# Blockwise attention feeding routed experts on one Trainium2 core: disjoint output views for the scatters, queries stored contiguous in blocks of 64, second-layer weights in row pairs

## The chip, the cores and the metric

The program runs on one core of one Trainium2 chip. The engines of a core are TensorE (PE; its weight loads are shown apart, as PEld), VectorE (DVE), ScalarE (ACT), GpSimd (POOL) and SyncE (SP); 16 DMA engines move data between the memory in HBM and the on-chip memory SBUF. The metric is device time in microseconds (us), the median of several executions.

## The reference

The first part is attention over 8 batches and 8 heads with 576 tokens of 64 numbers, causal by blocks of 64 tokens. The second part sends each of the 4608 rows of the attention output through one of eight small two-layer networks (the experts), chosen by an integer per row.

```python
def _attn_ref(q, k, v):                       # 8, 8, 576, 64
    scores = (1.0 / np.sqrt(D)) * np.matmul(q, k.transpose(0, 1, 3, 2))
    mask = (pos[:, None] // 64) >= (pos[None, :] // 64)
    scores = np.where(mask, scores, -1e9)
    attn = np.exp(scores - max);  attn = attn / (sum + 1e-09)
    return np.matmul(attn, v)

x = attn_out.transpose(0, 2, 1, 3).reshape(4608, 512)
for e in range(8):                            # w1: 8, 512, 1024   w2: 8, 1024, 512
    mask = domain_id == e
    out[mask] = np.maximum(x[mask] @ w1[e], 0.0) @ w2[e]
```

## The kernel before

**Attention stage.** The work goes in 32 pairs (8 batches times 4 pairs of heads). Queries, keys and values come in as float32, two batches at a time after the first, by DMAs that POOL issues; POOL casts them to float16 (L112, L116, L130). Query token t of a batch, after the first 64, is loaded as `(p j)` with j = 4: a partition holds four neighbouring tokens. `emit_T` transposes each head's four slices on PE into a PSUM tile `PT` (L311), so that PT holds the tokens of slice j side by side: column n of slice j is token 4n + j. DVE copies PT into the SBUF tile `QK`. The keys are put back into token order by that copy (L317). The queries are copied as they lie, slice after slice (L315), and token order is made each time they are read:

```python
def q_cols(QK, h, n0, n1):
    return QK[h, 0].rearrange("p (j n) -> p n j", j=4)[:, n0 // 4 : n1 // 4, :]
```

Neighbouring elements of such a read lie 128 elements, 256 bytes, apart. The last 64 keys and the first 64 queries of a batch are a "tail", transposed apart by `emit_tail` (L329) into `QT`.

For every pair `emit_G` makes three groups of score matmuls: group 0 has 512 query columns, group 1 has 384 and 128, group 2 has 256 (all L341, by `mm_qk`) and the twelve 64-column edge blocks (L369). Each matmul exists twice, once for either head of the pair, on partitions 0 to 63 and 64 to 127, with outputs in different PSUM banks (or, for the edges, different partitions). ACT makes the exponential of each group (L347). The tile `ps` that the groups write has two buffers. `emit_P` and `emit_Q` then multiply the exponentials of the pair before by the values (L397, L402) into the one tile `po`; a column of ones gives the row sums; DVE takes the reciprocal (L418) and scales `po` into `x` (L419). On PE the order of a pair is: group 0, the transposes for the pair after next, group 1, P of the pair before, group 2, Q of the pair before. `po` has one buffer, so the next P waits for L419. All engine queues are in the order of the code; there is no planner.

SP stores `x` to `x_rows` in HBM, one batch at a time. Between the pairs, `loads(p)` lets POOL cast and issue DMAs: at p = 3 the casts of the next keys and the weight loads of expert 0, at p = 4 the cast of the tail tile `th` of batch 2, and so on; `emit_tail` for batch b + 1 is in pair 4b + 2. DVE meanwhile works out, a step per pair, where each row goes (`routing`, `inverse`); the 36 matmuls of `inverse` are L216. The result is `tok`: a list of rows for each expert, 40 lists of 128, in `tok[:, 0]` as numbers of output rows and in `tok[:, 1]`, limited to 4607, as rows to gather.

**Expert stage.** Each expert has room for 640 rows, in five blocks. POOL gathers the blocks by indirect DMAs (L539); PE transposes them (L551), multiplies by w1 (`mm1`, L565, 64 matmuls of 320 columns), ACT applies the relu (L570), PE multiplies by w2 (`mm2`, L579, 40 matmuls of 512 columns), DVE copies each block's result to one of six `osb` buffers (L583) and POOL scatters it by an indirect DMA into the rows of `out` (L584). The weights are cast to float16 by the DMAs that bring them (L135, L138), four pieces for each matrix. All scatters name the whole tensor `out` as their destination. POOL's queue in expert e is: five gathers for expert e + 2, then for each block its scatter and two weight pieces for expert e + 3 (for e up to 4). A last loop (L631) serves experts with over 640 rows; it runs no round on these inputs.

Of the kernel before, what the change touches and what calls it, by code (L numbers as in the profile page):

```python
# [7 lines left out]

F32 = mybir.dt.float32
# [8 lines left out]
def kernel(  # L18
# [10 lines left out]
    nc = tc.nc  # L29
# [107 lines left out]
    def w2_piece(w2h, w2_e, i):  # L137
        nc.gpsimd.dma_start(  # L138
            out=w2h[:, 2 * i : 2 * i + 2],
            in_=w2_e[256 * i : 256 * i + 256, :].rearrange("(c p) f -> p c f", p=128))  # L140

    def load_w1(pool, bufs, w1_e):
        w1h = pool.tile([128, 4, Fdim], F16, name="w1h", tag="w1h", bufs=bufs)
# [42 lines left out]
    def inverse(sb, pp, tag, pbufs, ncols, base, tok):  # L186
        ub = sb.tile([128, NJ], F16, name="ub", tag="ub")
        nc.vector.tensor_scalar(
            out=ub[:], in0=u_f[:], scalar1=base, scalar2=None, op0=ALU.subtract)
        inv = sb.tile([128, 3, ncols], F32, name="inv", tag="inv")  # L190
        yield
        for hf in range(2):
            js = slice(NH * hf, NH * hf + NH)
            L = sb.tile([128, 128, NH], F16, name="L", tag="L")
            Hh = sb.tile([128, 3, ncols, NH], F16, name="Hh", tag="Hh")
            sh = [128, ncols, NH]
            nc.vector.tensor_tensor(
                out=Hh[:, 0], in0=iota_x[:, 0:ncols],
                in1=ub[:, js].unsqueeze(1).to_broadcast(sh), op=ALU.is_equal)
            nc.vector.tensor_scalar(  # L200
                out=Hh[:, 1], in0=Hh[:, 0], scalar1=p_f[:, 0:1], scalar2=None,
                op0=ALU.mult)
            nc.vector.tensor_tensor(
                out=Hh[:, 2], in0=Hh[:, 0],
                in1=iota_h[:, js].unsqueeze(1).to_broadcast(sh), op=ALU.mult)
            yield
            for m in range(0, 128, 64):
                nc.vector.tensor_tensor(
                    out=L[:, m : m + 64], in0=iota_x[:, m : m + 64],
                    in1=lo_h[:, js].unsqueeze(1).to_broadcast([128, 64, NH]),  # L210
                    op=ALU.is_equal)
                yield
            ps = pp.tile([128, 512], F32, name=tag, tag=tag, bufs=pbufs)
            pv = ps[:, 0 : 3 * ncols].rearrange("p (a c) -> p a c", a=3)
            for j in range(NH):
                nc.tensor.matmul(out=pv, lhsT=L[:, :, j], rhs=Hh[:, :, :, j],  # L216
                                 start=(j == 0), stop=(j == NH - 1))
# [10 lines left out]
        nc.vector.tensor_tensor(  # L228
            out=tok[:, 0], in0=inv[:, 0], in1=inv[:, 1], op=ALU.add)
        nc.vector.tensor_scalar(  # L230
            out=tok[:, 1], in0=tok[:, 0], scalar1=float(N - 1), scalar2=None,
            op0=ALU.min)
        yield

    def slot_col(asb, r_f, d_f, w, u, nm):
# [68 lines left out]
    def emit_T(p):  # L304
        b, hp = divmod(p, HP)
        PT = aps.tile([128, 2, 4, 128], F16, name="PT", tag="PT", bufs=2)
        QK = asb.tile([128, 2, 512], F16, name="QK", tag="QK", bufs=3)
        for s, src in enumerate((qh[b % 4], kh[b % 4])):
            for j in range(4):
                for i in range(2):  # L310
                    nc.tensor.transpose(  # L311
                        out=PT[64 * i : 64 * i + 64, s, j, :],
                        in_=src[:, 2 * hp + i, 64 * j : 64 * j + 64],
                        identity=identh[:])
        nc.vector.tensor_copy(  # L315
            out=QK[:, 0].rearrange("p (j n) -> p j n", j=4), in_=PT[:, 0])
        nc.vector.tensor_copy(  # L317
            out=QK[:, 1].rearrange("p (n j) -> p n j", j=4),
            in_=PT[:, 1].rearrange("p j n -> p n j"))
        return QK  # L320

    def q_cols(QK, h, n0, n1):
        return QK[h, 0].rearrange("p (j n) -> p n j", j=4)[:, n0 // 4 : n1 // 4, :]


    def emit_tail(QT, b):
        PT = aps.tile([128, HP, 2, 64], F16, name="PT", tag="PT", bufs=2)
        for g in range(HP):
            nc.tensor.transpose(  # L329
                out=PT[:, g].rearrange("p s n -> p (s n)"),  # L330
                in_=th[b % 4][:, 2 * g : 2 * g + 2, :].rearrange("p h d -> p (h d)"),
                identity=identh[:])
# [5 lines left out]
    def mm_qk(o, QK, c):  # L338
        for i in range(2):
            h = slice(64 * i, 64 * i + 64)  # L340
            nc.tensor.matmul(  # L341
                out=o[:, i].rearrange("p (n j) -> p n j", j=4),
                lhsT=QK[h, 1, 128 * c : 128 * c + 128],
                rhs=q_cols(QK, h, 128 * c, 512), start=True, stop=True)

    def emit_exp(o, i):
        nc.scalar.activation(out=o, in_=i, func=AF.Exp, scale=0.125)  # L347
# [1 line left out]
    def emit_G(g, st):  # L349
        QK = st["QK"]  # L350
        ps = aps.tile([128, 2, 512], F32, name="ps", tag="ps", bufs=2)
        if g == 0:
            mm_qk(ps[:], QK, 0)
            st["A1"] = asb.tile([128, 2, 512], F16, name="A1", tag="A1", bufs=2)
            emit_exp(st["A1"][:], ps[:])
        elif g == 1:
            mm_qk(ps[:, :, 0:384], QK, 1)
            mm_qk(ps[:, :, 384:512], QK, 3)
            st["A2"] = asb.tile([128, 2, 512], F16, name="A2", tag="A2", bufs=2)
            emit_exp(st["A2"][:], ps[:])  # L360
        else:
            mm_qk(ps[:, :, 0:256], QK, 2)
            for m in range(6):
                n0 = 128 * min(m, 4)
                c0 = 256 + 64 * (m % 3)
                QT = st["QT"][:, st["p"] % HP]
                for i in range(2):
                    h = slice(64 * i, 64 * i + 64)
                    nc.tensor.matmul(  # L369
                        out=ps[h, m // 3, c0 : c0 + 64].rearrange(  # L370
                            "p (n j) -> p n j", j=4),
                        lhsT=QK[h, 1, n0 : n0 + 64] if n0 < 512 else QT[h, 1],
                        rhs=q_cols(QK, h, n0 - 64, n0) if n0 else QT[h, 0].rearrange(
                            "p (n j) -> p n j", j=4),
                        start=True, stop=True)
# [182 lines left out]
    def mm1(xT, w1h):  # L558
        hT = msb.tile([128, 8, CAP], F16, name="hT", tag="hT", bufs=2)
        hw = CAP // 2  # L560
        for fc in range(8):
            ph = mps.tile([128, 2, 512], F32, name="ph", tag="ph", bufs=2)
            for dc in range(4):
                for i in range(2):
                    nc.tensor.matmul(  # L565
                        out=ph[:, i, 0:hw],
                        lhsT=w1h[:, dc, 128 * fc : 128 * fc + 128],
                        rhs=xT[:, dc, hw * i : hw * i + hw],
                        start=(dc == 0), stop=(dc == 3))
# [5 lines left out]
    def mm2(hT, w2h, tok, todo=()):  # L575
        for blk in range(NB):
            po = mps.tile([128, 512], F32, name="po", tag="po", bufs=2)
            for fc in range(8):
# [3 lines left out]
            osb = msb.tile([128, DM], F32, name="osb", tag="osb", bufs=6)  # L582
            nc.vector.tensor_copy(out=osb[:], in_=po[:])  # L583
            nc.gpsimd.indirect_dma_start(  # L584
                out=out,
                out_offset=bass.IndirectOffsetOnAxis(
                    ap=tok[:, 0, blk : blk + 1], axis=0),
                in_=osb[:], in_offset=None, bounds_check=N - 1, oob_is_err=False)
# [3 lines left out]
    def tok_of(e):  # L592
        return tok0[:, :, NB * e : NB * e + NB]
# [21 lines left out]
    for e in range(E):  # L615
# [14 lines left out]
    n_it = nc.values_load(n_i[0:1, 0:1], min_val=0, max_val=E * (N // CAP))  # L630
    with tc.For_i(0, n_it, 1) as it:  # L631
# [9 lines left out]
        for f in todo:  # L641
            f()
        hT = mm1(transpose_x(gather(tok)), w1h)
        mm2(hT, w2h, tok)


# [28 lines left out]
```

## Time and profile before

| | us |
|---|---|
| median of 3 runs | 456.5 (453.43 to 457.91) |
| the profiled execution | 451.2 |
| its span, first to last instruction | 449.2 |
| PE busy | 370.9 (83%) |
| POOL busy | 220.0 (49%) |
| DVE busy | 158.3 (35%) |
| ACT busy | 144.8 (32%) |

The row of an engine in the timeline gives the start, the busy time of a merged group of instructions, engine, line, operation, output and inputs, shape and count, and in brackets how long the engine sat idle before it and what ended that. A start minus the start of the next group is the time that a group holds the engine; matmuls are pipelined, so that the duration shown of one is longer than the time to the next. The gathers begin at 229.13 us; what lies before is the attention stage, what lies behind the expert stage.

### The profile page before, as it was taken

How to read it: one execution, taken by the hardware profiler on the slowest of the kernel's cores; microseconds unless marked ns; L12 is line 12 of the kernel's file. 1: busy time of each engine (PE TensorE's matmuls, PEld its weight loads, DVE VectorE, ACT ScalarE, POOL GpSimd, SP SyncE). 2: the span in 40 equal slices, each digit the busy share in tenths (PEclk: the TensorE clock that was granted, in tenths of full speed). 3: DMA queues.
4: the chain of work that ended last, by engine and by line, in shares of the span. 5: the costliest groups of instructions: out<-in, count | busy, mean ns of one | idle time of the engine just before them, and what ended most of it. 6: DMA issues, size and time to landing. Idle time of an engine off the chain costs nothing. (4 is left out here: it accounts for less than half of the span.)

```text
span 449.2 us, 7273 instructions
## 1 busy us (share of the span) xinstructions
PE 370.9 (83%) x3014; PEld 210.1 (47%) x3014; DVE 158.3 (35%) x302; ACT 144.8 (32%) x196; POOL 220.0 (49%) x252
## 2 busy tenths in 40 slices
PE   2879969999999999999718999897978969699300
PEld 1445535655555555555405565554453625446100
DVE  7849764444444434353210415121212122131100
ACT  1535433525454544455303150413040401304000
POOL 9869787745853100000048655647575464632220
PEclk9999999999999999999999999999896959989855
DMA  9999998953999010101035999694957869311210
GB/s 240 284 251 294 224 212 288 269 135 89 350 197 198 1 55 1 54 2 54 1 99 117 191 221 181 142 175 126 180 132 165 140 145 177 105 72 64 77 70 13
DMA packets 33635, 65.03 MB, mean 145 GB/s; under 512 B 4734, under 2 KB 19582, under 8 KB 33600
## 3 DMA queue, kind: packets, MB, share of 16 engines
q0 software_dynamic: 25424, 57.42, 55.4%
q1 hardware_dynamic: 7376, 6.72, 5.4%
q8 instruction: 25, 0.41, 0.4%
q10 hardware_dynamic: 800, 0.39, 0.3%
q14 instruction: 10, 0.08, 0.1%
HBM read 67.15 MB, written 15.20 MB: 183 GB/s over the span
## 5 line engine op out<-in xcount | busy, mean ns | idle before, releaser
L347 ACT ACTIVATE A<-ps 128x1024 f16<-128x1024 f32 (+1 forms) x96 | 84.4, 881 | 117.0 <-PE ps L341 75.2
L570 ACT ACTIVATE hT<-ph 128x640 f16<-128x640 f32 x64 | 44.9, 703 | 145.8 <-PE ph L565 101.8
L341 PE MATMUL ps<-QK 64*128 64x512 f16 (+3 forms) x256 | 84.3, 703 | 0.0
L539 POOL DMA_INDIRECT xg<-x_rows,tok x40 | 40.6, 1015 | 83.7 <-DMA x_rows<-x 71.4
L584 POOL DMA_INDIRECT out_dram<-osb,tok x40 | 40.9, 1024 | 79.7 <-DMA out_dram<-osb,tok 26.7
L579 PE MATMUL po<-w2h,hT 128*128 128x512 f16 x320 | 78.8, 411 | 0.0
L565 PE MATMUL ph<-xT,w1h 128*128 128x320 f16 x512 | 73.0, 303 | 1.9 <-issue 1.7
L565 PEld LDWEIGHTS <-w1h 128*128 128x128 f16 x512 | 50.8, 99 | 23.9 <-issue 2.6
L402 PE MATMUL po<-vS,A 128*128 128x65 f16 x640 | 55.4, 248 | 0.0
L583 DVE COPY osb<-po 128x512 f32<-128x512 f32 x40 | 27.6, 691 | 73.4 <-PE po L579 40.4
L579 PEld LDWEIGHTS <-hT 128*128 128x128 f16 x320 | 33.3, 105 | 42.3 <-issue 11.3
L402 PEld LDWEIGHTS <-A 128*128 128x128 f16 x640 | 49.6, 135 | 0.9 <-issue 0.9
L397 PE MATMUL po<-VE,ATE 128*128 128x130 f16 x160 | 44.9, 297 | 1.3 <-DVE x L419 1.3
L554 DVE COPY xT<-pt 128x512 f16<-128x512 f16 x40 | 16.3, 423 | 76.9 <-PE pt L551 69.2
L551 PE MATMUL pt<-identh,xg 128*128 128x128 f16 x160 | 17.1, 243 | 28.5 <-DMA xg<-x_rows,tok 17.7
L418 DVE RECIPROCAL rc<-po 128x12 f32<-128x12 f32 x32 | 7.5, 233 | 84.5 <-PE po L397 84.5
L397 PEld LDWEIGHTS <-ATE 128*128 128x128 f16 x160 | 19.3, 121 | 31.7 <-issue 31.1
L130 POOL CAST vS<-vst 128x1024 f16<-128x1024 f32 (+1 forms) x21 | 18.7, 923 | 28.1 <-PE po L402 17.5
L419 DVE TENSOR_TENSOR x<-po,rc 128x768 f16<-128x768 f32 x32 | 30.6, 957 | 1.1
L122 POOL DMA_DIRECT2D vst<-in_v_dram x25 | 25.3, 1024 | 8.5 <-DMA qs<-in_q_dram 8.1
L311 PEld LDWEIGHTS <-qh 128*64 128x64 f16 x256 | 12.8, 158 | 34.0 <-issue 24.9
L311 PE MATMUL PT<-identh,qh 128*64 128x128 f16 x256 | 20.4, 314 | 8.2 <-DVE qh L112 8.2
(97 smaller groups left out, 334.8 us busy)
## 6 DMA issues: line engine op xcount, KB each, us to landing
w1h<-in_moe_w_dram POOLq DMA_DIRECT2D x32, 256.0 KB
w2h<-in_moe_w_dram POOLq DMA_DIRECT2D x32, 256.0 KB
qs<-in_q_dram POOLq DMA_DIRECT2D x3, 2048.0 KB
ks<-in_k_dram POOLq DMA_DIRECT2D x3, 2048.0 KB
vst<-in_v_dram POOLq DMA_DIRECT2D x12, 512.0 KB
x_rows<-x SPq DMA_DIRECT2D x8, 512.0 KB, 4.7
vst<-in_v_dram POOLq DMA_DIRECT2D x11, 256.0 KB
qs<-in_q_dram POOLq DMA_DIRECT2D x1, 1024.0 KB
```

Source lines behind the costliest of these rows:

```text
L311: nc.tensor.transpose(out=PT[64 * i : 64 * i + 64, s, j, :], in_=src[:, 2 * hp + i, 64 * j : 64 * j + 64], identity=identh[:])
L341: nc.tensor.matmul(out=o[:, i].rearrange("p (n j) -> p n j", j=4), lhsT=QK[h, 1, 128 * c : 128 * c + 128], rhs=q_cols(QK, h, 128 * c, 512) ...
L347: nc.scalar.activation(out=o, in_=i, func=AF.Exp, scale=0.125)
L397: nc.tensor.matmul(out=o[:, 1:131], lhsT=st["AE"][:, 128 * m : 128 * m + 128], rhs=VE[b % 2][:, m, hp, 1:131], start=True, stop=(m == 0))
L402: nc.tensor.matmul(out=o[:, 1 + 65 * i : 66 + 65 * i], lhsT=at_block(st, i, c, m), rhs=vS[b % 3][:, c, hp, 1 + 65 * i : 66 + 65 * i], star ...
L419: nc.vector.tensor_tensor(out=st["x"][:, :, 128 * hp : 128 * hp + 128].rearrange("p (b w) (i z) -> p b w i z", b=2, i=2), in0=pv[:, :, :, ...
L539: nc.gpsimd.indirect_dma_start(out=g[:, blk, :], out_offset=None, in_=xd, in_offset=bass.IndirectOffsetOnAxis(ap=tok[:, 1, blk : blk + 1], ...
L565: nc.tensor.matmul(out=ph[:, i, 0:hw], lhsT=w1h[:, dc, 128 * fc : 128 * fc + 128], rhs=xT[:, dc, hw * i : hw * i + hw], start=(dc == 0), s ...
L570: nc.scalar.activation(out=hT[:, fc].rearrange("p (i n) -> p i n", i=2), in_=ph[:, :, 0:hw], func=AF.Relu)
L579: nc.tensor.matmul(out=po[:], lhsT=hT[:, fc, 128 * blk : 128 * blk + 128], rhs=w2h[:, fc, :], start=(fc == 0), stop=(fc == 7))
L583: nc.vector.tensor_copy(out=osb[:], in_=po[:])
L584: nc.gpsimd.indirect_dma_start(out=out, out_offset=bass.IndirectOffsetOnAxis(ap=tok[:, 0, blk : blk + 1], axis=0), in_=osb[:], in_offset=N ...
```

## The change

Three edits go together.

1. `dram_disjoint_views(out, 40)` makes 40 views of the whole output which the framework takes to be disjoint. Each scatter of the expert stage names a view of its own; in the last loop the first five are used.
2. The copy of the queries out of PSUM stores each block of 64 tokens together, in it slice by slice: column 64m + 16j + n is token 64m + 4n + j. Score matmuls read and write these columns straight. The query tail is stored in the same order, in a copy of its own. The order of rows in `x`, and so in `x_rows`, is then permuted within each 64; `inverse` turns the row number r into (r & -64) + ((r & 3) << 4) + ((r >> 2) & 15) for the gather, with five more DVE operations on 40 columns. The scatter's row numbers stay as they were.
3. A piece of w2 (256 rows) is loaded with rows 2p and 2p + 1 on partition p, in place of rows p and 128 + p. The columns of w1 that are loaded into PE as weights are taken with a step of two to match.

```diff
+    outs = dram_disjoint_views(out, E * NB)
@@ w2_piece
-            in_=w2_e[256 * i : 256 * i + 256, :].rearrange("(c p) f -> p c f", p=128))
+            in_=w2_e[256 * i : 256 * i + 256, :].rearrange("(p r) f -> p r f", r=2))
@@ inverse
         nc.vector.tensor_scalar(
-            out=tok[:, 1], in0=tok[:, 0], scalar1=float(N - 1), scalar2=None,
+            out=rw[:, 0], in0=tok[:, 0], scalar1=float(N - 1), scalar2=None,
             op0=ALU.min)
+        (rw[:, 1] = (rw[:, 0] & 3) << 4;  rw[:, 2] = (rw[:, 0] >> 2) & 15;  rw[:, 0] &= -64)
+        yield
+        (rw[:, 1] += rw[:, 2];  tok[:, 1] = rw[:, 0] + rw[:, 1])
@@ emit_T
-            out=QK[:, 0].rearrange("p (j n) -> p j n", j=4), in_=PT[:, 0])
+            out=QK[:, 0].rearrange("p (m j n) -> p m j n", j=4, n=16),
+            in_=PT[:, 0].rearrange("p j (m n) -> p m j n", n=16))
@@ emit_tail
-        nc.vector.tensor_copy(out=QT[:], in_=PT[:])
+        nc.vector.tensor_copy(
+            out=QT[:, :, 0].rearrange("p g (j n) -> p g j n", j=4),
+            in_=PT[:, :, 0].rearrange("p g (n j) -> p g j n", j=4))
+        nc.vector.tensor_copy(out=QT[:, :, 1], in_=PT[:, :, 1])
@@ mm_qk
-                out=o[:, i].rearrange("p (n j) -> p n j", j=4),
-                lhsT=QK[h, 1, 128 * c : 128 * c + 128],
-                rhs=q_cols(QK, h, 128 * c, 512), start=True, stop=True)
+                out=o[:, i], lhsT=QK[h, 1, 128 * c : 128 * c + 128],
+                rhs=QK[h, 0, 128 * c : 512], start=True, stop=True)
@@ emit_G (edges)
-                        out=ps[h, m // 3, c0 : c0 + 64].rearrange(
-                            "p (n j) -> p n j", j=4),
+                        out=ps[h, m // 3, c0 : c0 + 64],
                         lhsT=QK[h, 1, n0 : n0 + 64] if n0 < 512 else QT[h, 1],
-                        rhs=q_cols(QK, h, n0 - 64, n0) if n0 else QT[h, 0].rearrange(
-                            "p (n j) -> p n j", j=4),
+                        rhs=QK[h, 0, n0 - 64 : n0] if n0 else QT[h, 0],
@@ mm1
-                        lhsT=w1h[:, dc, 128 * fc : 128 * fc + 128],
+                        lhsT=w1h[:, dc].rearrange(
+                            "p (c n r) -> p c r n", n=128, r=2)[:, fc // 2, fc % 2],
@@ mm2
-                out=out,
+                out=dst[blk],
...
-        mm2(hT, w2s[e], tok_of(e), todo)
+        mm2(hT, w2s[e], tok_of(e), outs[NB * e : NB * e + NB], todo)
```

More of the change, by code (lines that the diff above doesn't have):

```diff
@@ L6 @@
 from concourse._compat import with_exitstack
+from concourse.ap import dram_disjoint_views
 from concourse.masks import make_identity, make_upper_triangular
@@ L229, in inverse @@
             out=tok[:, 0], in0=inv[:, 0], in1=inv[:, 1], op=ALU.add)
+        rw = sb.tile([128, 3, ncols], I32, name="rw", tag="rw")
         nc.vector.tensor_scalar(
-            out=tok[:, 1], in0=tok[:, 0], scalar1=float(N - 1), scalar2=None,
+            out=rw[:, 0], in0=tok[:, 0], scalar1=float(N - 1), scalar2=None,
             op0=ALU.min)
+        nc.vector.tensor_scalar(
+            out=rw[:, 1], in0=rw[:, 0], scalar1=3, scalar2=4,
+            op0=ALU.bitwise_and, op1=ALU.arith_shift_left)
+        nc.vector.tensor_scalar(
+            out=rw[:, 2], in0=rw[:, 0], scalar1=2, scalar2=15,
+            op0=ALU.arith_shift_right, op1=ALU.bitwise_and)
+        nc.vector.tensor_scalar(
+            out=rw[:, 0], in0=rw[:, 0], scalar1=-64, scalar2=None,
+            op0=ALU.bitwise_and)
+        yield
+        nc.vector.tensor_tensor(
+            out=rw[:, 1], in0=rw[:, 1], in1=rw[:, 2], op=ALU.add)
+        nc.vector.tensor_tensor(
+            out=tok[:, 1], in0=rw[:, 0], in1=rw[:, 1], op=ALU.add)
         yield
@@ L573, in mm1, with mm2 @@
         return hT
-    def mm2(hT, w2h, tok, todo=()):
+    def mm2(hT, w2h, tok, dst, todo=()):
         for blk in range(NB):
@@ L643 @@
         hT = mm1(transpose_x(gather(tok)), w1h)
-        mm2(hT, w2h, tok)
+        mm2(hT, w2h, tok, outs[0:NB])
 _INS = ['q', 'k', 'v', 'moe_domain_id', 'moe_w1', 'moe_w2']
```

2 lines of the change are left out of this document (removed).

## The prediction

> **What bounds the kernel now.** I read the page first, then PE's timeline, then POOL's. Of the page: the span, the granted clock and the DMA share in 40 slices of 11.2 us.
>
> ```profile
> span 449.2 us, 7273 instructions
> PEclk9999999999999999999999999999896959989855
> DMA  9999998953999010101035999694957869311210
> DMA out_dram<-osb,tok 4%; POOL out_dram L584 0%; POOLq L630 0%; POOLq L584 0%
> ```
>
> The DMA engines are full or nearly so in the first eight slices (to 90 us) and again in many of slices 22 to 33; the clock dips only late. The chain that ended last holds nothing but scatters. PE's timeline for one pair in the middle of the attention stage:
>
> ```profile
> 173.78 1.02 PE L341 MATMUL ps<-QK 64*128 64x512 f16 x2
> 174.74 0.64 PE L311 MATMUL PT<-identh,qh 128*64 128x128 f16 x8
> ...
> 175.74 1.03 PE L341 MATMUL ps<-QK 64*128 64x384 f16 x4
> 176.70 0.29 PE L397 MATMUL po<-VE,ATE 128*128 128x130 f16 x1
> ...
> 177.80 0.60 PE L341 MATMUL ps<-QK 64*128 64x256 f16 x2
> 178.33 0.26 PE L369 MATMUL ps<-QT,QK 64*64 64x64 f16 x2
> 178.41 0.49 PE L369 MATMUL ps<-QK 64*64 64x64 f16 x6
> 178.73 0.39 PE L369 MATMUL ps<-QK,QT 64*64 64x64 f16 x4
> 179.05 0.29 PE L397 MATMUL po<-VE,ATE 128*128 128x130 f16 x1
> 179.14 0.65 PE L402 MATMUL po<-vS,A 128*128 128x65 f16 x8
> 179.59 0.30 PE L397 MATMUL po<-VE,ATE 128*128 128x130 f16 x1
> 179.82 1.02 PE L341 MATMUL ps<-QK 64*128 64x512 f16 x2
> ```
>
> No row has an idle time in brackets: PE is the bound here, at 179.82 − 173.78 = 6.04 us a pair. Of this the L341 groups hold 0.96 + 0.96 + 0.53 = 2.45 us, the edges 0.72. The whole attention stage is not so: DMA holds PE up early.
>
> ```profile
> 59.62 0.71 POOL L138 DMA_DIRECT2D w2h<-in_moe_w_dram  x1 [0.25 <-DMA vst<-in_v_dram]
> 60.32 0.62 POOL L116 CAST th<-ts 128x512 f16<-128x512 f32 x1
> 61.00 0.61 PE L329 MATMUL PT<-identh,th 128*128 128x128 f16 x4 [4.12 <-POOL th L116]
> 95.96 4.13 PE L216 MATMUL PT<-Hh,L 128*128 128x120 f16 x18
> 128.25 3.99 POOL L112 CAST kh<-ks 128x1024 f16<-128x1024 f32 x4 [4.24 <-DMA ks<-in_k_dram]
> ```
>
> At the end of pair 6 PE waits for a tail cast that POOL reaches only after issuing expert 0's weights behind a full DMA. In the expert stage POOL's and PE's rows:
>
> ```profile
> 229.13 1.10 POOL L539 DMA_INDIRECT xg<-x_rows,tok  x1 [71.40 <-DMA x_rows<-x]
> 386.69 0.99 POOL L539 DMA_INDIRECT xg<-x_rows,tok  x1 [0.30 <-issue]
> 434.66 0.98 POOL L584 DMA_INDIRECT out_dram<-osb,tok  x1 [2.52 <-DMA out_dram<-osb,tok]
> 438.16 0.98 POOL L584 DMA_INDIRECT out_dram<-osb,tok  x1 [2.52 <-DMA out_dram<-osb,tok]
> 238.53 10.26 PE L565 MATMUL ph<-xT,w1h 128*128 128x320 f16 x63 [0.25 <-issue]
> 259.27 8.86 PE L565 MATMUL ph<-xT,w1h 128*128 128x320 f16 x64
> 269.99 8.80 PE L579 MATMUL po<-w2h,hT 128*128 128x512 f16 x40
> 278.62 6.68 PE L565 MATMUL ph<-xT,w1h 128*128 128x320 f16 x48
> 391.30 0.40 PE L551 MATMUL pt<-identh,xg 128*128 128x128 f16 x4 [1.43 <-DMA xg<-x_rows,tok]
> 410.55 8.80 PE L579 MATMUL po<-w2h,hT 128*128 128x512 f16 x40
> ```
>
> A scatter starts 3.50 us after the one before (438.16 − 434.66), because it waits 2.52 us for that one to land. Everything behind it on POOL's queue waits too: the gathers, then PE's transposes (391.30), whose gaps let the clock fall. An expert without gaps takes 278.62 − 259.27 = 19.35 us. After PE's last matmul (419.35) a string of scatters is still to come.
>
> **The views.** Gathers show what indirect DMAs cost when none waits for the other: 0.99 + 0.30 = 1.3 us apart. An expert's POOL work is then 5 gathers and 5 scatters at 1.3 us and eight weight pieces, whose mean cost the groups by shape give:
>
> ```profile
> L138 POOL DMA_DIRECT2D w2h<-in_moe_w_dram x32 | 23.5, 756 | 7.1 <-DMA vst<-in_v_dram 4.9 <-DMA w2h<-in_moe_w_dram 2.2
> L135 POOL DMA_DIRECT2D w1h<-in_moe_w_dram x32 | 17.9, 580 | 0.9 <-DMA vst<-in_v_dram 0.5 <-DMA w2h<-in_moe_w_dram 0.4
> L565 PEld LDWEIGHTS <-w1h 128*128 128x128 f16 x512 | 50.8, 99 | 23.9 <-issue 2.6
> L216 PEld LDWEIGHTS <-L 128*128 128x128 f16 x36 | 5.1, 144 | 2.4
> L315 DVE COPY QK<-PT 128x512 f16<-128x512 f16 x32 | 13.5, 422 | 16.7 <-PE PT L311 16.4
> L317 DVE COPY QK<-PT 128x512 f16<-128x512 f16 x32 | 21.8, 680 | 0.0
> L419 DVE TENSOR_TENSOR x<-po,rc 128x768 f16<-128x768 f32 x32 | 30.6, 957 | 1.1
> L347 ACT ACTIVATE A<-ps 128x1024 f16<-128x1024 f32 x64 | 65.3, 1023 | 75.2 <-PE ps L341 75.2
> ```
>
> That is 13 + 4 × 0.76 + 4 × 0.58 = 18.4 us, under PE's 19.35, so PE takes over as the bound. From the first gather, mm1 of expert 1 starts after 259.27 − 229.13 = 30.1 us; six experts at 19.35 follow, and the last without transposes takes 8.86 + 8.80 = 17.7: PE ends 163.9 us after the first gather. Today it is 419.35 − 229.13 = 190.2. Gain 26.3. Behind PE's end stand 449.2 − 419.35 = 29.9 us today; after, the last copy and issue (an estimate of 1.3 us from the 1.3 us issue step) and what follows the start of the last scatter today, 449.2 − 438.16 = 11.0: 12.3 us. Gain 17.6. Together 43.9.
>
> What is late next is DMA. The digits of slices 20 to 39 sum to 106 tenths of 11.2 us: 119 us at least, about 130 if each digit drops half a tenth. The weights follow ten gathers, 13 us after the first, and nearly all is due when mm1 of expert 7 starts, 163.9 − 17.7 = 146 us after the first gather: 13 + 130 = 143, just in time; at nine tenths of the rate it would be 157, 11 us late. Scatters will also queue behind weights, and a copy into `osb` waits for the scatter six before it. I allow 4 us (bounds 0 and 11) and count 40.
>
> **The queries.** L216 reads its moving operand with a step of 36 bytes and has no partner on other partitions: 18 in 4.13 us, 0.23 us per 120 columns, 1.9 ns a column. L341, stepping 256 bytes, takes 0.96 us for a pair of 512 columns: also 1.9 ns, for both heads at once. The two heads thus run side by side, and what they pay for is the step. A contiguous read is seen in L579: 8.80 / 40 = 0.22 us per 512 columns, 0.43 ns each. The pair's 512 + 384 + 128 + 256 = 1280 columns would take 0.55 us. If the heads ran one after the other at full speed, which nothing here excludes, 1.10. I add 0.15 to the first for weight loads that short matmuls no longer cover, and take 0.70: a gain of 1.75 (bounds 1.35 and 1.90). The edges: the contiguous two (L369 from QT) hold PE 0.08 us, the six strided ones 0.32, 0.107 for two; five pairs of them gain 0.03 each, rounded down to 0.1 in all.
>
> That last 0.1 has a rule against it. The six take 0.32 / 6 = 53 ns each, the contiguous ones 40. The Trainium skill, "TensorE: Matmul & The Clock Gate", section "Part 2: What happens when you issue a matmul", has the sequencer spend about 62 ns on each matmul when decoding in software, by which twelve edges would stay near 0.74 us and the 25 pairs below gain 2.5 us less. The rows are already under that, so the sum keeps the 0.1.
>
> A pair then takes 6.04 − 1.85 = 4.2 us. Covers that could fail: ACT has four exponentials a pair, two of 1.02 and two smaller, so under 4.1 us, below 4.2; DVE's turn of `po` takes 0.96 and a reciprocal of twelve columns, while group 0, transposes (1.00) and group 1 come to about 1.5, so P just does not wait. The new query copy costs 0.42 (as L315) to 0.68 (as L317, every element with a step); it moves in runs of 16, and DVE would have 2 × 0.68 + 0.96 and the reciprocal, some 2.5 us, a pair even so. All of this hides under PE.
>
> Only pairs 7 to 31 gain: pairs before end at the 61.00 row, and the cast that it waits for hangs on the DMA, which is full from the start. 25 × 1.85 = 46.3 us. PE, faster, waits there up to 4.12 + 7 × 1.85 = 17 us in place of 4.12 and starts again slowly: the first mm1, after the pause between the stages, took 10.26 against 8.86, so 1.4 us are lost. Later loads keep up: the key cast for batches 6 and 7 ends at 132.2 today (128.25 + 3.99), and pair 22, which transposes the first of them, would start at about 61.5 + 15 × 4.2 + 8 (L216 twice) + 2 (tails) = 135.
>
> **The five DVE operations** in `inverse` cost 0.2 to 0.8 us each by their kind, and in a pair where DVE also has 2.5 us to do they could delay P: 1 us, bounds 0 and 4. They are done long before the gathers.
>
> ```profile
> L295 DVE TENSOR_SCALAR lo_i<-rit 128x36 int32<-128x36 int32 x1 | 0.8, 784 | 0.0
> ```
>
> **Row pairs of w2.** Its issue should fall from 756 to w1's 580, since each partition now has one run in place of two: 0.18 × 4 for an expert, off POOL's 18.4, hidden under PE; in front of the 60.32 cast, up to the 0.7 us of issue and some of the wait for ring space (4 us, the size of PE's stall) could go. I take 0, bounds −4 and 0. As to transfer, each row of w2 is 2 KB of float32 already; by the Trainium skill, "DMA: Bandwidth & Descriptors", section "Specifications", 512 bytes suffice for the line rate, by which the pairs give nothing, and the rows here cannot separate the two. The strided weight loads of w1: L565's takes 99 ns in a couple of 8.86 / 64 = 138 ns; even L216's, with its step of 36 bytes, takes 144. I take 0, bounds 0 and 512 × 6 ns = 3 us.
>
> **The sum.** 449.2 − 40 − 46.3 + 1.4 + 1 = 365.3 us span; the profiled execution adds 2.0 (451.2): 367.3. The median of the runs shown stands at 456.5 / 451.2 = 1.012 of that execution: 372 us.
>
> **Rivals.** *DMA binds the expert stage*: many slices stand at nine already, while w2 and w1 come three experts ahead; the allowance becomes 11, 379 us. *The heads take turns at full speed*: 25 × 0.4 = 10 us less gain, 382; the strided pairs, side by side, speak against it. *The scatters still wait* (the wait comes from somewhere else than the shared name): only the attention's 46.3 gained, 2.4 lost, some 412; the gathers, free of such waits today, speak against it. *The step is not what slows L341*: only the views gain, 416; the match with L216 speaks against it. *Slower than before*: the stepped weight loads of w1 bind mm1. A couple costs the larger of 138 ns and the load; the gains of 84 us are gone when 512 × (load − 138) reaches 84 us, at a load of 302 ns, and the time is 461 at 311 ns. It decides above 302; L216's 144 speaks against it.
>
> **The numbers.** Forecast as summed 0.55; DMA-bound 0.20; heads in turn 0.10; scatters still waiting 0.07; step harmless 0.05; slower 0.015; the rest, about no change, 0.015. The forecast's own bounds go from 372 − 4 (no DMA stall) − 4 (w2) − 1 (DVE) − 25 × 0.15 (the queries' upper bound) = 359 to 372 + 3 (DVE) + 3 (loads of w1) = 378. The runs shown spread by some 4 us. The range that holds eight in ten takes in both rivals next to it, the two together (372 + 7 + 10 = 389) and that spread with the upper bounds: 355 to 397. About 1% is what a measurement of this kernel can tell from no change: faster 0.97, same 0.015, slower 0.015.
>
> **What would show it.** L341's three groups near 0.7 us in a pair and pairs 4.2 apart; PE idle before the pair 6 tail for over ten us; scatters on POOL 1.3 us apart with no bracket naming `out_dram`; transposes without waits for xg; PE's end some 164 us after the first gather and the span's end 12 us later. It would be wrong if DVE's copies wait for `out_dram`, if ACT or `po` gates the pairs, or if L565 loads grow past 138 ns.

## The result, and the profile after

The changed kernel takes 348.57 us (median; 347.5 to 349.57) against 454.97 us before (452.41 to 457.91): a ratio of 0.7659, 95% interval 0.76 to 0.7719. It is faster, as forecast, but by 106 us and not by 84: 372 had been predicted and 355 was the lower end of the range. The profiled execution took 349.14 us. Medians here are of all runs of a kernel, ratios and their intervals only of those within 1.5% of its fastest. From the page of the changed kernel: the span, the granted clock and the DMA share in 40 slices (of 8.7 us now), and two groups of instructions.

```profile
span 347.1 us, 7286 instructions
PEclk9996885559788996999857999999999999999996
DMA  7999999999938999122225999899998989601121
POOLq L648 0%; POOL out_dram L602 0%
L414 PE MATMUL po<-VE,ATE 128*128 128x130 f16 x160 | 34.6, 241 | 18.0 <-DVE x L436 15.2
L142 POOL DMA_DIRECT2D w2h<-in_moe_w_dram x32 | 17.4, 562 | 9.2 <-DMA vst<-in_v_dram 6.2 <-DMA w2h<-in_moe_w_dram 2.9
```

The chain of landing scatters that ended the span before is gone. DMA is now at eight tenths or more in 14 of the first 16 slices (to 139 us) and again over most of the expert stage. The granted clock, which had read nine up to slice 30 before, now dips from the fourth slice on. The changed lines have moved: the scores are L361 (was L341), the edges L388 (L369), the scatters L602 (L584), P·V L414 and L419 (L397 and L402).

PE's timeline of the changed kernel for one late pair (start, duration, line, idle before it in brackets):

```profile
154.68 0.39 PE L361 MATMUL ps<-QK 64*128 64x512 f16 x2
155.00 0.41 PE L330 MATMUL PT<-identh,qh 128*64 128x128 f16 x8
155.24 0.39 PE L330 MATMUL PT<-identh,kh 128*64 128x128 f16 x8
155.57 0.39 PE L361 MATMUL ps<-QK 64*128 64x384 f16 x4
...
156.69 0.28 PE L361 MATMUL ps<-QK 64*128 64x256 f16 x2
156.90 0.22 PE L388 MATMUL ps<-QT,QK 64*64 64x64 f16 x2
...
157.28 0.41 PE L419 MATMUL po<-vS,A 128*128 128x65 f16 x8
...
157.67 0.39 PE L361 MATMUL ps<-QK 64*128 64x512 f16 x2
```

A pair takes 157.67 − 154.68 = 2.99 us, where 6.04 stood before and 4.2 were forecast. The scores fell as expected: group 0 from 0.96 to 0.32, group 2 from 0.53 to 0.21. But the transposes, which the change does not touch, fell as well: the queries' eight, from one row's start to the next, took 0.24 us here, and both sets took 155.57 − 155.00 = 0.57 against 1.00 before. That is the surprise of this case, and the experiments turn on it.

PE's rows and POOL's of the changed kernel, around the expert stage:

```profile
174.72 1.10 POOL L556 DMA_INDIRECT xg<-x_rows,tok  x1 [34.53 <-DMA x_rows<-x]
205.00 8.86 PE L582 MATMUL ph<-xT,w1h 128*128 128x320 f16 x64
224.35 5.87 PE L582 MATMUL ph<-xT,w1h 128*128 128x320 f16 x42
329.79 8.80 PE L597 MATMUL po<-w2h,hT 128*128 128x512 f16 x40
339.59 0.98 POOL L602 DMA_INDIRECT out_dram<-osb,tok  x1 [0.74 <-DVEq L649]
```

The first gather comes at 174.72 (229.13 before): attention gave 54.4 us. PE ends at 329.79 + 8.80 = 338.59, which is 163.9 us after the first gather, and an expert takes 224.35 − 205.00 = 19.35 us. The last scatter waits 0.74 us for DVE (the one before it, at 337.87, the same time for DVE's copy into `osb`) and no longer for the scatter before it. The span ends 8.5 us after PE, where it was 29.9.

### The profile page after: what moved, and what is told of

Its sections match the earlier page's. It is cut to its first block, busy times and chain, and to the rows that moved or that the text cites. A ratio compares the mean times of both kernels' runs of the same rounds, so it can differ in the third digit from the quotient of the medians.

```text
span 347.1 us, 7286 instructions
## 1 busy us (share of the span) xinstructions
PE 277.5 (80%) x3014; PEld 177.8 (51%) x3014; DVE 165.8 (48%) x315; ACT 141.4 (41%) x196; POOL 213.5 (62%) x252
## 5 line engine op out<-in xcount | busy, mean ns | idle before, releaser
L597 PE MATMUL po<-w2h,hT 128*128 128x512 f16 x320 | 70.4, 379 | 0.0
L602 POOL DMA_INDIRECT out_dram<-osb,tok x40 | 40.8, 1020 | 39.7 <-DVE osb L601 26.1
L597 PEld LDWEIGHTS <-hT 128*128 128x128 f16 x320 | 30.9, 98 | 36.0
L414 PE MATMUL po<-VE,ATE 128*128 128x130 f16 x160 | 34.6, 241 | 18.0 <-DVE x L436 15.2
L419 PEld LDWEIGHTS <-A 128*128 128x128 f16 x640 | 34.3, 107 | 16.9 <-issue 15.9
L361 PE MATMUL ps<-QK 64*128 64x512 f16 (+3 forms) x256 | 39.3, 346 | 1.2 <-ACT ATE L366 0.7
L419 PE MATMUL po<-vS,A 128*128 128x65 f16 x640 | 39.2, 208 | 0.0
L126 POOL DMA_DIRECT2D vst<-in_v_dram x25 | 25.1, 1014 | 10.5 <-DMA qs<-in_q_dram 9.1
L330 PE MATMUL PT<-identh,qh 128*64 128x128 f16 x256 | 16.1, 261 | 10.7 <-DVE qh L116 8.6
L134 POOL CAST vS<-vst 128x1024 f16<-128x1024 f32 (+1 forms) x21 | 18.2, 897 | 10.0 <-DMA vst<-in_v_dram 7.0
L142 POOL DMA_DIRECT2D w2h<-in_moe_w_dram x32 | 17.4, 562 | 9.2 <-DMA vst<-in_v_dram 6.2
L337 DVE COPY QK<-PT 128x512 f16<-128x512 f16 x32 | 21.8, 680 | 0.0
L414 PEld LDWEIGHTS <-ATE 128*128 128x128 f16 x160 | 16.5, 103 | 10.1 <-issue 7.8
```

The lines of the kernel that those rows point to most:

```text
L126: nc.gpsimd.dma_start(out=vst[0:n, c, o, :], in_=v[b0:b1, :, 128 * c : 128 * c + n, :].rearrange("b h p d -> p (b h) d"))
L361: nc.tensor.matmul(out=o[:, i], lhsT=QK[h, 1, 128 * c : 128 * c + 128], rhs=QK[h, 0, 128 * c : 512], start=True, stop=True)
L414: nc.tensor.matmul(out=o[:, 1:131], lhsT=st["AE"][:, 128 * m : 128 * m + 128], rhs=VE[b % 2][:, m, hp, 1:131], start=True, stop=(m == 0))
L419: nc.tensor.matmul(out=o[:, 1 + 65 * i : 66 + 65 * i], lhsT=at_block(st, i, c, m), rhs=vS[b % 3][:, c, hp, 1 + 65 * i : 66 + 65 * i], star ...
L597: nc.tensor.matmul(out=po[:], lhsT=hT[:, fc, 128 * blk : 128 * blk + 128], rhs=w2h[:, fc, :], start=(fc == 0), stop=(fc == 7))
L602: nc.gpsimd.indirect_dma_start(out=dst[blk], out_offset=bass.IndirectOffsetOnAxis(ap=tok[:, 0, blk : blk + 1], axis=0), in_=osb[:], in_off ...
```

## The experiments

### Each part alone: the layout without the views, the views without the layout

The first theory was that the two large parts act in separate stages: the layout in attention, the views in the expert stage. Its rival was that one of them has effects in both stages. The first kernel keeps the new order of the queries and drops the views and the row pairs:

```diff
-                out=dst[blk],
+                out=out,
-            in_=w2_e[...].rearrange("(p r) f -> p r f", r=2))
+            in_=w2_e[...].rearrange("(c p) f -> p c f", p=128))
```

> The changed kernel with the output named whole again in every scatter and w2 as before: only the query layout of the change is left. If the two large edits add up, the first gather starts near 174.7 us as in the changed kernel and the expert stage takes 220 us as in the kernel before: a span of about 395 us. In a full-clock pair the transposes of four query slices for both heads (8 matmuls) hold PE 0.25 us as in the changed kernel. If instead the faster attention stage needed the views or the w2 loads, the first gather starts later than 180 us.

It took 401.53 us in the one execution made of it, with a span of 399.4 where about 395 was expected. The first gather comes at 175.66, within 1 us of the full change, and the scatters wait for each other as before. POOL's timeline of this kernel:

```profile
388.40 0.98 POOL L601 DMA_INDIRECT out_dram<-osb,tok  x1 [2.52 <-DMA out_dram<-osb,tok]
```

The other kernel is the one before with the views alone:

```diff
+    outs = dram_disjoint_views(out, E * NB)
-                out=out,
+                out=dst[blk],
```

> The kernel before with the disjoint views alone. The attention stage stays as before (first gather near 229 us, a pair 6.04 us, 8 transposes 0.43 us); the expert stage goes at PE's pace: PE ends 164 us after the first gather, the span ends 8.5 us later, about 401 us. If the expert stage of the changed kernel also needed the w2 pairs to keep DMA ahead, PE shows waits for weights or gathers there and the span is above 404 us.

It took 411.09 us, again in one execution, with a span of 409.2 where about 401 was expected. The first gather stays at 229.93 and PE ends 166.9 us after it; in the expert stage PE waits 2.9 us in one place for gathered rows. PE's timeline of this kernel shows the pair as it was before:

```profile
149.94 1.03 PE L343 MATMUL ps<-QK 64*128 64x512 f16 x2
150.90 0.64 PE L313 MATMUL PT<-identh,qh 128*64 128x128 f16 x8
151.32 0.64 PE L313 MATMUL PT<-identh,kh 128*64 128x128 f16 x8
...
155.98 1.03 PE L343 MATMUL ps<-QK 64*128 64x512 f16 x2
```

The pair takes 6.04 us and one set of transposes 0.42. So the cheaper transposes come with the layout and not with the views, and nearly all of attention's gain is the layout's (53.5 of 54.4). The two parts alone give 49.8 and 40.0 us of span; together with the row pairs they give 102.1. The 12.3 us more than the sum are mostly in the expert stage. With the layout alone that stage is 3.6 us longer than before. With the views alone it is 6.9 us longer than with the whole change. About 4 of these 6.9 us lie behind PE's end, and the w2 runs below come back to them. All of this rests on single executions, in a session in which the kernel before spread from 441.2 to 457.35 us; differences of a few us are not certain.

### Why unchanged work became cheaper: the clock

The theory now was that PE's clock stood at half through the whole attention stage before, because its activity there was low while stepped reads held it, and that contiguous reads let the clock rise. The rival was that the transposes were cheaper for a reason of their own, such as less contention for SBUF without the stepped reads beside them. The test keeps the kernel before with all its stepped reads and puts four contiguous matmuls of 512 columns ahead of each of the three score groups. Their output is overwritten by the scores, so they add work and change nothing else:

```diff
+    def filler(ps, QK, n=2):
+        for _ in range(n):
+            for i in range(2):
+                h = slice(64 * i, 64 * i + 64)
+                nc.tensor.matmul(out=ps[:, i], lhsT=QK[h, 1, 0:128],
+                                 rhs=QK[h, 1, 0:512], start=True, stop=True)
```

> The kernel before, with work added: before every score group four contiguous matmuls of 512 columns (two for each head), overwritten by the real ones. Clock theory (reads with a step of 256 bytes hardly count as activity, so PE ran the attention stage at half clock): if the added matmuls count, 8 transposes fall from 0.43 to 0.25 us, the stepped reads stay at 1.9 ns a column, and a pair takes 2.45 + some 2.0 + 1.3 for the filler = 5.8 us, no slower than 6.04 although it has more to do. If the clock does not come up, the filler costs 2.6 us and a pair takes 8.6. Rate theory (only the stepped reads themselves were slow): the transposes stay at 0.43 us and the pair takes 7.3 to 8.6 us.

It took 458.84 us. PE's timeline of this kernel (the filler is L350):

```profile
38.91 0.61 PE L350 MATMUL ps<-QK 64*128 64x512 f16 x4
39.35 1.02 PE L341 MATMUL ps<-QK 64*128 64x512 f16 x2
40.30 0.41 PE L311 MATMUL PT<-identh,qh 128*64 128x128 f16 x8
40.55 0.39 PE L311 MATMUL PT<-identh,kh 128*64 128x128 f16 x8
...
45.49 1.02 PE L341 MATMUL ps<-QK 64*128 64x512 f16 x2
```

One set of transposes takes 40.55 − 40.30 = 0.25 us beside stepped reads that are all still there and still take 0.95 us. Three fillers of 0.44 us are 1.32 us more work in a pair, and the pair takes 45.49 − 39.35 = 6.14 us (5.8 was expected), 0.10 more than without them. Contention for SBUF falls with this. More work of the contiguous kind made the rest faster, as a clock does that rises with activity. The same trace also has both states on record. Between 73 and 77 us the granted clock reads 0.50: a filler takes 0.83 us (72.93 to 73.76), a set of transposes 0.42 (74.74 to 75.16), and the stepped 512 columns between them 0.98. Between 79 and 81 us it reads 1.00, and a filler takes 0.44 (80.86 to 81.30). The DMA engines are as full in the one stretch as in the other (1.02 and 1.04).

The trace of the changed kernel shows the same switch within 10 us. First the windows (busy times, then granted clock, DMA share and GB/s), then PE's timeline in them:

```profile
86.00:90.00 4.00, 3.78 (x65) 2.85 (x65) 3.93 (x9) 2.00 (x3) 3.40 (x3) 1.00 1.05 269
94.00:98.00 4.00, 4.00 (x53) 2.48 (x47) 1.40 (x4) 2.48 (x4) 1.04 (x1) 0.50 0.63 125
```

```profile
88.70 4.11 PE L220 MATMUL PT<-Hh,L 128*128 128x120 f16 x18
...
93.28 0.64 PE L330 MATMUL PT<-identh,qh 128*64 128x128 f16 x8
93.71 0.64 PE L330 MATMUL PT<-identh,kh 128*64 128x128 f16 x8
```

L220 holds PE for 4.11 us with reads of a 36-byte step. Behind it the clock reads 0.50, with PE busy without a gap, and a set of transposes takes 93.71 − 93.28 = 0.43, which is the price it had in every pair before. L220 itself took 4.13 us before, and L341's stepped 512 columns 0.96 before and 0.95 with the filler: a stepped read costs the same at either clock. The kernel before, however, shows this window row for its attention stage:

```profile
100.00:229.00 129.00, 122.24 (x1230) 68.75 (x1229) 49.84 (x95) 60.27 (x80) 29.09 (x34) 1.00 0.35 92
```

The granted clock reads 1.00 there, over transposes at 0.43. The changed kernel's trace does the same near its start, ahead of its first dip (which is recorded at about 27 us): a window at 1.00, and in it transposes at 0.64 us a row, as in every pair before, where the late pair has 0.39.

```profile
10.00:20.00 10.00, 6.58 (x77) 3.76 (x78) 8.77 (x17) 6.16 (x8) 7.73 (x10) 1.00 1.04 263
```

```profile
16.48 0.64 PE L330 MATMUL PT<-identh,kh 128*64 128x128 f16 x8
```

So a reading ahead of the first recorded dip is no evidence of the clock; the duration of a row that is known at both rates is. The Trainium skill, "TensorE: Matmul & The Clock Gate", "Part 1: The HAM clock gate (the "warmup" mystery)", has the clock at half by default and doubled after some 3.4 us of sustained activity, with 427 and 216 ns for 512 columns. On the two rates the rows here agree: the transposes, 512 columns for each head, take 0.43 us at half clock, and L597 takes 8.80 / 40 = 0.22 us for 512 columns. That part of the page does not speak of stepped moving reads, with which PE was busy here and still at half clock.

### Which steps cost what

Two variants of the changed kernel read the queries with a step in some score groups only. They take the same columns in another order, so their scores belong to other queries, and only their time is of use. In the first, group 0 keeps the old 256-byte step:

```diff
+    def mm_qk0(o, QK):
...
+                lhsT=QK[h, 1, 0:128],
+                rhs=QK[h, 0].rearrange("p (j n) -> p n j", j=4),
...
-            mm_qk(ps[:], QK, 0)
+            mm_qk0(ps[:], QK)
```

> The changed kernel, but the 512-column group 0 reads its queries with the 256-byte step again (the columns are then in another order, so that the scores belong to other queries); groups 1 and 2 and the edges stay contiguous. Group 0 goes from 0.32 to 0.96 us. Clock theory: if 512 of 1280 columns are few enough, the clock stays up and a pair late in the stage takes 3.0 + 0.64 = 3.65 us; if they are enough to bring it down, 8 transposes go from 0.25 to 0.43 us and the pair takes about 5. Rate theory: 3.65 us with the transposes at 0.25, as nothing else could change.

It took 359.27 us. PE's timeline of this kernel:

```profile
148.42 1.02 PE L361 MATMUL ps<-QK 64*128 64x512 f16 x2
149.37 0.41 PE L330 MATMUL PT<-identh,qh 128*64 128x128 f16 x8
149.62 0.39 PE L330 MATMUL PT<-identh,kh 128*64 128x128 f16 x8
149.94 0.39 PE L370 MATMUL ps<-QK 64*128 64x384 f16 x4
150.26 0.23 PE L423 MATMUL po<-VE,ATE 128*128 128x130 f16 x1
...
150.91 0.28 PE L370 MATMUL ps<-QK 64*128 64x256 f16 x2
151.12 0.22 PE L397 MATMUL ps<-QT,QK 64*64 64x64 f16 x2
...
151.89 1.02 PE L361 MATMUL ps<-QK 64*128 64x512 f16 x2
```

The stepped group takes 0.95 us, but the transposes stay at 0.25: one stepped group of three does not bring the clock down, and a pair takes 3.47 us. The gain of the layout has two halves, then: the step, paid by each column that has one, and the clock, which all of PE's other work pays.

The second variant steps by 4, 8 and 16 bytes in groups 0, 1 (its 384 columns) and 2:

```diff
+                rhs=QK[h, 0, 128 * c : 512].rearrange("p (n r) -> p r n", r=r),
-            mm_qk(ps[:], QK, 0)
+            mm_step(ps[:], QK, 0, 2)
-            mm_qk(ps[:, :, 0:384], QK, 1)
+            mm_step(ps[:, :, 0:384], QK, 1, 4)
-            mm_qk(ps[:, :, 0:256], QK, 2)
+            mm_step(ps[:, :, 0:256], QK, 2, 8)
```

> The changed kernel with small steps in the query reads (columns in another order, so that scores belong to other queries): group 0 reads its 512 columns with a step of 4 bytes, the 384 columns of group 1 with 8, the 256 of group 2 with 16. If what matters is whether two reads in a row fall in one 16-byte line, groups 0 and 1 keep their 0.32 and 0.33 us and group 2 goes from 0.21 to about 0.5. If any step costs, groups 0 and 1 rise towards 0.96.

It took 354.72 us. PE's timeline of this kernel:

```profile
146.19 0.40 PE L361 MATMUL ps<-QK 64*128 64x512 f16 x2
146.51 0.41 PE L330 MATMUL PT<-identh,qh 128*64 128x128 f16 x8
...
147.09 0.50 PE L361 MATMUL ps<-QK 64*128 64x384 f16 x2
147.40 0.24 PE L370 MATMUL ps<-QK 64*128 64x128 f16 x2
147.57 0.23 PE L423 MATMUL po<-VE,ATE 128*128 128x130 f16 x1
...
148.22 0.61 PE L361 MATMUL ps<-QK 64*128 64x256 f16 x2
148.76 0.22 PE L397 MATMUL ps<-QT,QK 64*64 64x64 f16 x2
```

The 4-byte step takes 146.51 − 146.19 = 0.32 us for 512 columns, as much as without a step. The 8-byte step makes group 1 take 147.57 − 147.09 = 0.48 us, where the variant above shows 0.32 (150.26 − 149.94): its 384 columns take 0.31, 0.8 ns each. No price had been expected there. The 16-byte step takes 0.54 for 256 columns, as much as 256 bytes did before (0.53) and against 0.21 without one (151.12 − 150.91). The Trainium skill, "Advanced Engine Details and Errata", "SBUF Cachelines", has 16-byte lines in SBUF and asks for at least two hits on a line to absorb the access latency. That agrees with 4 and 16 bytes. If two hits are taken to be enough, it does not agree with 8, where two columns share a line and a price is still paid, and the measurement decides.

### The row pairs of w2

The theory on record was that they are worth nothing; the rival, that they relieve the queues. The kernel is the changed one with w2's rows single and w1's columns in order, run twice, the second time beside the changed kernel on one chip:

```diff
-            in_=w2_e[...].rearrange("(p r) f -> p r f", r=2))
+            in_=w2_e[...].rearrange("(c p) f -> p c f", p=128))
-                        lhsT=w1h[:, dc].rearrange(
-                            "p (c n r) -> p c r n", n=128, r=2)[:, fc // 2, fc % 2],
+                        lhsT=w1h[:, dc, 128 * fc : 128 * fc + 128],
```

> The changed kernel with w2 and the weight columns of w1 as before. If the w2 edit is worth nothing because PE is the bound, the time stays within 1% of 348.6 us, with w2's issue on POOL back at some 750 ns from 562 and L565-type weight loads at 99 ns either way. If the pairs keep DMA or POOL ahead, it is slower by more than 3 us, with waits of PE for weights, gathers or po.

> The changed kernel itself, so that the next three stand beside it on the same chip: a median of 345 to 351 us as before, first gather at 174 to 176 us, w2's issue at some 560 ns. If the wait of about 15 us that ScalarE showed in the expert stages of the kernel without row pairs and of the one with late weights belongs to those kernels, it isn't found here; if it comes and goes with any kernel, the single times spread by 6 us or more here as well.

> The change with its first and second part but w2's rows single and w1's columns in order, again. If the row pairs are worth what the first look suggested (a wait of about 6 us and a tail about 4 us longer), the median is 6 to 12 us above the changed kernel's on this chip, 355 to 360, and the profile shows an expert stage that the weights hold up. If they are worth nothing and the first run met a wait that comes by chance, it is within 3 us of the changed kernel's, 346 to 351.

The first time it took 359.93 us (353.93 to 362.61), and its profile had a wait of 3.61 us in one expert stage; with the kernel before at 441.2 to 457.35 us in the same session, no ratio can be given. The second time it took 354.56 (353.17 to 354.94; ratio to before 0.7775, 0.7732 to 0.7819) without such a wait, beside 350.31 for the changed kernel (348.84 to 351.62; 0.7687, 0.7641 to 0.7732). The two intervals just touch, but no run of the one kernel is as fast as any of the other, so some 4 us are lost without the pairs. Where are they? PE's timelines show that PE starts its last mm2 at 329.82 and 329.70, with 8.80 us to go: nothing is gained up to PE's end, and the spans of the two profiles, 351.3 and 346.9, differ behind it. The waits of the SP queue, for the kernel with single rows and then for the changed one (waiting line, releaser, us in total, times, longest):

```profile
SPq L687 <- PEq L687: 6.0, 2, 5.5
```

```profile
SPq L688 <- PEq L688: 2.9, 2, 2.4
```

At the end of the program, behind all the work, SP waits for PE's sequencer, and this wait is 3.1 us longer with single rows. It is 5.5 us in every profile here of a kernel without the pairs (the one before, both parts alone, the filler), and 2.4 with them, but 4.7 in both profiles of the kernel below that has the pairs and loads expert 0's weights at pair 20. So no gain in the pairs' transfers is seen, and the wait does not go by the pairs alone; what PE's sequencer does in that time the trace does not show, and it stays open.

### Expert 0's weights later: the best version

At the end of pair 6 PE waits 8.69 us in the changed kernel, because POOL reaches the tail's cast only after it has issued expert 0's weights at pair 3. If that order is the cause, issuing them later removes the wait:

```diff
-        if p == 3:
+        if p == 20:
```

> The changed kernel with the weight loads of expert 0 moved from pair 3 to pair 20. If PE's 8.7 us wait for the tail cast of batch 2 and the later waits come from DMA work and POOL time that these loads put ahead of them, the wait falls under 4 us, the loads of the later batches start 5 to 12 us earlier and the time falls to 337 to 344 us. If the stage is held by something else (DVE, or the loads of queries, keys and values alone), the wait only moves and the time stays above 345.

> Expert 0's weights requested at pair 20 and not at pair 3, again, beside the changed kernel on the same chip. If the wait for V and the tail's Q and K at pair 6 (8.7 us) was theirs, the first gather comes at about 165 us and the median is 4 to 9 us below the changed kernel's, 339 to 344.

> The same loads at pair 12, between the transfers of attention's first third and the casts of the expert weights behind them. If all that matters is that they leave the queue before pair 6, the first gather comes at about 165 us as with pair 20 and the median at 339 to 344. If late loads push the later ones back and the waits for VectorE (4.3 and 4.8 us near 40 and 53 us with pair 20) follow from that, they are shorter here and it is 2 to 4 us better, 336 to 341.

At pair 20 it took 346.08 us in the first run (340.85 to 348.5; ratio 0.754, 0.7469 to 0.7611) and 341.49 in the second (341.21 to 342.96; ratio 0.75, 0.7458 to 0.7542), beside 350.31 for the changed kernel on that chip: 2.5% faster than the change, and the best of all. The wait at pair 6 is gone but for 0.21 us, and the first gather comes at 163.62, where the changed kernel has 173.91 in that session. Some of these 10.3 us are given back at the end, where the span ends 11.6 us after PE and not 8.4. At pair 12 it took 350.38, no better than the changed kernel and not the 339 to 344 expected, and its first gather came at 174.58. PE's waits from 100 to 160 us, for pair 12 and then for pair 20, show why:

```profile
PE PT L330 <- POOL qh L116: 7.6, 1, 7.6
PE po L414 <- DVE x L436: 5.8, 3, 5.3
PE PT L330 <- POOL kh L116: 4.6, 1, 4.6
PE PT L346 <- POOL th L120: 1.9, 1, 1.9
```

```profile
PE po L414 <- DVE x L436: 12.5, 7, 3.7
```

Issued at 12, the weights delay the queries and keys of a later batch, and the wait that is gone at pair 6 comes back as 7.6 + 4.6 + 1.9 = 14.1 us of waits for POOL's casts. Issued at 20, they no longer stand in front of anything that PE waits for. In the first run's profile of pair 20 an expert stage had a wait of 3 us at PE, as in the first run with single rows. The second run of either kernel had none, so it does not belong to the edit, and its cause was not found.

## Why the prediction was right and wrong

**The views: right.** PE was to end 163.9 us after the first gather; it ends 338.59 − 174.72 = 163.9 us after it, with the forecast 19.35 us for an expert. Two terms were mis-sized. The 4 us allowed for DMA were not needed. The tail, forecast at 12.3 us, is 8.5: its last scatter starts 1.0 us after PE's end, close to the estimate of 1.3, but what follows that start takes 7.5 us and not the 11.0 taken over from the trace before. The SP wait shows 3.1 us of this difference. With the views alone the tail was 409.2 − 396.9 = 12.3 us, as forecast, so what is below it is not the views'.

**The queries: the mechanism right, the pair's price wrong.** That the step and not the heads' order sets the price holds: contiguous heads run side by side, and the scores fell to 0.32 + 0.32 + 0.21 = 0.85 us (0.70 was forecast; the 0.32 of group 1 is read in the variant with one stepped group). The step that failed is "A pair then takes 6.04 − 1.85 = 4.2 us". It left the other 3.5 us of a pair (6.04 − 2.45 − 0.1) at the durations of the trace before, under a granted clock that read 1.00. They were durations at half clock, and the pair takes 2.99 us. Of the 3.05 us gained, 1.60 are the scores', and 1.45 are work that the sum left as it was or nearly so: the transposes, P and Q, and the edges, which fell from 0.72 to 0.31 us (156.90 to 157.21) where 0.1 was forecast. A warning stood among the rows quoted there. L402's eight matmuls of 65 columns, on all 128 partitions and so with no partner beside them, took 179.59 − 179.14 = 0.45 us, 0.87 ns a column, while the same trace had 0.43 ns in L579. Now they take some 0.24 us (157.52 − 157.28 on PE's timeline), 0.46 ns a column.

**Only part of that came through.** At 2.99 us, 25 pairs would have gained 76 us, and attention gained 54.4. What stands against the other 22 us are the pairs that PE ran at half clock after its pauses and behind L220, a wait of 8.69 us at pair 6 (forecast as "over ten"; 4.12 before), and PE's waits for DVE's turn of `po`, 15.2 us in the page's row against 1.3 before, of which 8.6 come after pair 6. Their shares were not measured apart. That P "just does not wait" did not hold for the shorter pair. Late in the stage PE is busy 7.90 and ACT 7.49 of 8 us, so the next bound is close:

```profile
150.00:158.00 8.00, 7.90 (x169) 5.73 (x168) 6.68 (x15) 7.49 (x12) 0.00 (x0) 1.00 0.02 7
```

**The five DVE operations: about right.** They take 0.17 to 0.52 us each, 1.26 us together. They stand in a stretch where PE then waits 3.77 us for DVE (105.90), close to the bound of 4, but they hold only a part of it. The longest operation there is not one of the five: the limit to 4607 (now L235), which the kernel before has too, took 2.48 us in this execution, 0.18 before, and 0.18 again in the repeat of the changed kernel, where PE's wait at this place was 1.69 us. Why one operation takes so different times is open.

**Row pairs of w2: open.** Their issue fell from 756 to 562 ns (580 was forecast) and w1's strided weight loads stayed at 99 ns, both as expected. The 4 us that are lost without them are as much as the bound given, but at a place that no step named. That POOL waits for ring space, as the prediction has it, no run shows: the rows name the DMA of the values.

**The sum.** The span was forecast at 365.3 and is 347.1. Of the 18.2 us, 10.5 are attention (54.4 against 46.3 − 1.4 − 1 = 43.9), 4 the DMA allowance and 3.8 the tail. The factor of 1.012 for the median added 4.7 us that were not there: the median is 0.6 us below the profiled execution. The range was too narrow at its lower end, because its bounds varied only the costs of what the change touches and none of what it leaves alone.

**The rivals.** None came true. DMA is fuller but not late, heads do not take turns, the scatters no longer wait, the step is what slows the scores, and w1's loads never bind.

## What to carry to other kernels

Before a trace's duration is used for work that a change leaves alone, compare it with the same kind of work elsewhere in the trace: a row that costs twice as much per column says that PE may stand at half clock there, whatever the clock's own line reads ahead of its first dip. A moving operand with a step can cost twice over, once for its own columns and, as in the kernel before, once more in the clock of everything around it, so make the operand contiguous where it is copied anyway, or keep the step at 4 bytes for two-byte elements. And when a stage is made shorter, look at what its queue issues ahead of the next cast: moving eight weight loads from pair 3 to pair 20 was worth another 9 us, and to pair 12 nothing.

## What was not expected of the hardware

- Stepped moving reads cost 1.9 to 2.1 ns a column at the steps of 16, 36 and 256 bytes measured here, 0.8 ns at 8 bytes and nothing at 4 (0.32 us for 512 columns of both heads, as contiguous), and 4.11 against 4.13 us for the same 18 matmuls at two clocks.
- PE busy with such reads can be granted half its clock: 0.50 right behind 4.11 us of them. What share of them it takes is open. With the filler they are 2.4 of 6.14 us and the clock stays up; before, 2.45 of 6.04 us, and it was down. At half clock a filler takes 0.83 us, so by an estimate stepped reads are there 2.45 of 6.04 + 3 × 0.83 = 8.5 us of such a pair, which could be why that kernel comes out of half clock and the one before does not; no run tests it.
